# Routing attention with an activated FFN: cluster masks on VectorE and values in fours for half of the head pairs

## The chip, the cores and the metric

One NeuronCore of a Trainium2 chip runs the whole program. The metric is device time in microseconds, the median of several runs of the same kernel. Lower is better.

## What is computed

The attention block groups queries and keys of each head by their nearest centroid (16 per head) and lets a query see only keys of its own cluster. Its output, 3072 tokens of 512 features, goes through an FFN with a hard-swish. Everything is fp32.

```python
q_assign = np.argmax(np.einsum('bhsd,hcd->bhsc', q_n, c_n), axis=-1)      # B, H, S, D = 4, 8, 768, 64
k_assign = np.argmax(np.einsum('bhsd,hcd->bhsc', k_n, c_n), axis=-1)      # 16 clusters
mask = q_assign[:, :, :, None] == k_assign[:, :, None, :]
scores = np.where(mask, scale * np.matmul(q, k.transpose(0, 1, 3, 2)), -1000000000.0)
attn = np.exp(scores - np.max(scores, axis=-1, keepdims=True))
attn = attn / (np.sum(attn, axis=-1, keepdims=True) + 1e-09)
x = np.matmul(attn, v)                       # then (B, S, H*D) -> 3072 x 512
h = x @ w_in                                 # 512 x 2048
g = h * np.clip(h + 3.0, 0.0, 6.0) / 6.0
out = g @ w_out                              # 2048 x 512
```

## The kernel before

**Attention.** The 32 heads are handled as 16 pairs; the two heads of a pair (t = 0, 1) lie beside each other. A pair has 12 steps n: two halves hf of 384 queries, and in each half six chunks j of 128 keys. 192 steps in all, walked two at a time (r = n mod 12 is the place in the pair). A step's work:

- Scores (scores_part, L371). For each head the product of 128 keys and 384 queries over 64 features is laid on 64 of the array's rows, so the two heads lie side by side in the array; the result is keys by queries in one of two PSUM tiles ps. A second pair of bf16 matmuls, on the tile xm, adds the mask: xm holds one-hots of the query's cluster, and minus 2^60 for each cluster that is not the key's, so that a product over clusters is 0 for a match and minus 2^60 otherwise.
- Exponential (L387), ScalarE, from ps to a tile ex of 2 x 384 fp32 for both heads. Four buffers of ex.
- Key sums (L391, L394), GpSimd: the ex of the six chunks are added into acc. The first chunk of a half (j = 0) has no add.
- Values (attn_v, L398): v of the chunk times ex, each head on 64 columns of the array, accumulated over j in the one PSUM tile pv. After j = 5 ScalarE copies it to num (L410).
- Division (divide, L416) once a half: TensorE sums acc over the keys with a matrix of ones (pd, L425), VectorE takes the reciprocal (L429) and multiplies num (L430); what is stored of it and two ScalarE sums over it (in_range) wait in a list until the end of the next walk.

Values run two steps behind scores (lag_v = 2), so two values follow two scores in every walk. The tiles of the next pair are made during this one (prep_items, L680): three groups of transposes of q and k (turn), the products with the centroids (cluster_scores), their transposes and the one-hots by VectorE (route), and two groups of six transposes of one-hots that ScalarE copies to xm (route_turn). In the second half of the kernel all of these and pd share one PSUM buffer, that of the pool psum_t.

**FFN.** It runs by blocks of 256 tokens, 12 blocks. All but the first block's first product use a seven-product scheme of Strassen's kind on halves of the operands. A block has 15 items: eight ups (halved, L577) and seven downs (L629). An up makes seven partial products in two PSUM tiles, uX and uY, of a pool with two buffers; VectorE combines them (L603, L596, six instructions), ScalarE lifts (L453), VectorE clips (clip, L456), and after every second up four sums of the gated tiles are made by GpSimd, or by VectorE after the last (gated_sums, L575). The clip of an up is kept in the list ending and issued by finish() in the middle of the next up, between the work on uX and that on uY. In block 1 alone, first_sums (L507) makes four sums of w_in per up on VectorE; later blocks load them. A down is 16 matmul instructions of 256 columns or 32 in the first two; some end in adds to y on VectorE (L627).

**Order.** The order of every queue is written out by hand (manual_schedule, L717 on). In a walk come two scores, two values, a division where one is due, and then the fill: FFN items taken from a list, and between them the steps of the next pair's preparation, one after each item. items_by (L707) says how many FFN items should be done by step n: 8 by step 96, then 56 for every 48 steps. Up to step 96 (DECODED) VectorE and ScalarE also decode the weights beside the attention. After step 192 about 60 items are left, which run by themselves.

Of the kernel before, what the change touches and what calls it, by code (L numbers as in the profile page):

```python
# [17 lines left out]
C = 16  # L18
P = 128
# [97 lines left out]
def fast_path(ctx, tc, ok, q, k, v, centroids, moe_w_in, moe_w_out, out):  # L117
# [13 lines left out]
    rtp = pool("rtp", 1)  # L131
    smallp = pool("smallp", 1)
    expp = pool("expp", 4)
# [10 lines left out]
    decp = decoding.enter_context(tc.tile_pool(name="decp", bufs=2))  # L144
    psum_s = pool("psum_s", 2, space=PSUM)
# [20 lines left out]

    st = {}
    later = []

# [86 lines left out]
    cen = const.tile([P, D], F32, name="cen")  # L256
    parity = const.tile([P, 2], F32, name="parity")

    def constants():
# [10 lines left out]
        nc.gpsimd.memset(one_hot, 0.0)  # L270

# [4 lines left out]
    def centroid_norm():  # L276
        cn = unit_rows(nc, smallp, cen, D)
# [3 lines left out]
        wide = smallp.tile([P, 2, D], F32, name="cenwide")  # L281
# [40 lines left out]
    def route(g):  # L322
# [26 lines left out]
        later.append(count)  # L349

    def route_turn(g, part):
# [7 lines left out]
        nc.scalar.activation(out=dst, in_=po, func=ACT.Copy, scale=-FAR if part else 1.0)  # L359

# [10 lines left out]
    def scores_part(n, x, first):  # L371
        g, hf, j = where(n)
        for t in range(2):
            r = slice(t * D, (t + 1) * D)
            nc.tensor.matmul(  # L375
                st["ps", n][:, t, 0:HALF], lhsT=x[r, NCH + j],
                rhs=x[r, hf * NHC : (hf + 1) * NHC], start=first, stop=not first,
            )

    def scores(n):  # L380
        g, hf, j = where(n)
        if ("ps", n) not in st:
            scores_qk(n)
        scores_part(n, st["xm", g], False)
        sc = st.pop(("ps", n))[:, :, 0:HALF]
        ex = expp.tile([P, 2, HALF], F32, name="ex")
        nc.scalar.activation(out=ex, in_=sc, func=ACT.Exp, scale=SM_SCALE)  # L387
        st["ex", n] = ex
# [140 lines left out]
    def ffn_items(b):  # L529
# [47 lines left out]
        def halved(b, m, u, i, g):  # L577
# [28 lines left out]
            finish()  # L606
# [8 lines left out]
            lift(sx, g)  # L615
            ending.append(lambda: (clip(g, sx, g), gated_sums(i)))
# [63 lines left out]
    def prep_items(g, r):  # L680

        if g >= NPAIR:
            return []
        return {
            0: [lambda: turn(g, 0), lambda: turn(g, 1)],
            2: [lambda: turn(g, 2)],
            4: [lambda: cluster_scores(g)],
            6: [lambda: route(g)],
            8: [lambda: route_turn(g, 0)],
            10: [lambda: route_turn(g, 1)],  # L690
# [23 lines left out]
    fill, checks = [], []  # L714
    done = 0

    with tc.manual_schedule():  # L717
# [18 lines left out]
        for n in range(0, total + lag_d + 2, 2):  # L736
            g, r = divmod(n, per_pair)
            for i in (n, n + 1):
                if i < total:
                    scores(i)  # L740
            for i in (n - lag_v, n - lag_v + 1):
                if 0 <= i < total:
                    attn_v(i)
            m = n - lag_d + 1
            if m >= 0 and m % NCH == NCH - 1:
                later.append(divide(m))
# [416 lines left out]
```

## Time and profile before

| | |
|---|---|
| median of 3 runs | 1046.78 us (1046.28 to 1048.92) |
| the profiled execution: its own time | 1050.08 us |
| its span | 1048.3 us |
| steps 0 to 95 | to about 253 us |
| steps 96 to 191 | about 253 to 838 us |
| FFN items alone | about 838 us to the end |

| busy in the span | PE | PE weight loads | DVE | ACT | POOL |
|---|---|---|---|---|---|
| us | 1013.2 | 740.9 | 587.8 | 387.5 | 406.4 |

The stages are found by the starts of the exponentials. A row of the profile gives a line of the kernel, an engine, an operation and its tiles as output<-inputs. Rows of the timeline give start and duration in us; a row with x4 is four instructions in a row. A matmul row's duration reaches beyond the start of the next, since matmuls are pipelined: the pitch is read from the starts.

### The profile page before, as it was taken

To read this page: it belongs to the slowest core of one execution; us is meant where nothing else is said; L and a number is where in the kernel's file an instruction comes from. 1 tells how busy PE (TensorE), PEld (TensorE's weight loads), DVE (VectorE), ACT (ScalarE), POOL (GpSimd) and SP (SyncE) were. 2 spreads that over 40 slices of the span, in tenths; PEclk is the share of its full clock that TensorE was granted. 3 is DMA by queue.
4 is the path that set the end of the run, shared out by engine and by line. 5 is a ranking of instruction groups with operands and counts; after the bars stand their busy time and mean duration, and the time that the engine had idled before them with its cause. 6 is when DMAs were issued, how large, how long until landed. Compare 5 with 4: busy or idle time off the path is not lost.

```text
span 1048.3 us, 16637 instructions
## 1 busy us (share of the span) xinstructions
PE 1013.2 (97%) x6560; PEld 740.9 (71%) x6560; DVE 587.8 (56%) x1117; ACT 387.5 (37%) x764; POOL 406.4 (39%) x315
## 2 busy tenths in 40 slices
PE   8999989999998999999999999999999999999996
PEld 4444445546767778677777777777778798989995
DVE  4899987868477247246246345345245373727270
ACT  6888866674223233223223233233223111102010
POOL 3777657664234235135234235235334220303030
PEclk9999999999999999999999999999999999999999
DMA  6455554531043223223322232333032051414120
GB/s 164 107 141 142 161 143 111 141 84 46 31 118 104 54 81 89 53 66 84 73 71 88 64 89 64 71 94 96 3 91 86 1 144 34 142 42 140 51 61 25
DMA packets 107176, 90.34 MB, mean 86 GB/s; under 512 B 78416, under 2 KB 88656, under 8 KB 107088
## 3 DMA queue, kind: packets, MB, share of 16 engines
q1 hardware_dynamic: 106944, 89.15, 31.2%
q8 instruction: 54, 0.88, 0.3%
q14 instruction: 34, 0.28, 0.1%
q10 hardware_dynamic: 144, 0.03, 0.0%
HBM read 73.43 MB, written 15.73 MB: 85 GB/s over the span
## 4 chain that ended last, share of the span: by engine, by line
PE 76%; DVE 8%; ACT 2%; issue 1%; DMA 1%; SPq 1%; DVEq 0%; ACTq 0%
PE Y L620 16%; PE uY L585 13%; PE X L620 12%; PE ps L375 10%; PE uX L585 10%; PE pv L404 9%; PE ph L540 3%; DVE rcp L429 2%; PE pd L425 1%; DVE sx L596 1%; PE pqk L302 1%; DVE num L430 1%; DVE g_sb L456 1%; PE pcs L315 1%; SPq L191 1%
## 5 line engine op out<-in xcount | busy, mean ns | idle before, releaser
L394 POOL TENSOR_TENSOR acc<-acc,ex 128x768 f32<-128x768 f32 x128 | 239.6, 1872 | 226.8 <-ACT ex L387 220.9
L575 POOL TENSOR_TENSOR g_sb<-g_sb 128x256 f32<-128x256 f32 x144 | 105.9, 756 | 219.2 <-DVE g_sb L456 216.4
L453 ACT ACTIVATE sx<-g_sb,half_c 128x512 f32<-128x512 f32 x88 | 63.5, 722 | 304.7 <-DVE g_sb L596 304.7
L387 ACT ACTIVATE ex<-ps 128x768 f32<-128x768 f32 x192 | 146.4, 803 | 75.4 <-PE ps L375 75.1
L375 PE MATMUL ps<-xf 64*128 64x384 f32 x768 | 165.5, 509 | 4.0 <-ACT ex L387 4.0
L404 PE MATMUL pv<-ex,vt 128*64 128x384 f32 x768 | 145.1, 499 | 0.0
L391 POOL TENSOR_TENSOR acc<-ex 128x768 f32<-128x768 f32 x32 | 59.0, 1842 | 161.9 <-ACT ex L387 161.9
L429 DVE RECIPROCAL rcp<-pd 128x384 f32<-128x384 f32 x32 | 81.8, 2555 | 57.8 <-PE pd L425 57.8
L627 DVE TENSOR_TENSOR y<-y,Y 128x256 f32<-128x256 f32 x48 | 20.2, 420 | 157.8 <-PE Y L620 157.0
L404 PEld LDWEIGHTS pv<-ex,vt 128*64 128x64 f32 x768 | 46.6, 136 | 80.1 <-issue 75.8
L375 PEld LDWEIGHTS ps<-xf 64*128 64x128 f32 x768 | 63.1, 186 | 46.1 <-issue 28.8
L585 PE MATMUL uX<-xb,w_in_sb 128*128 128x128 f32 x704 | 93.8, 277 | 0.0
L620 PE MATMUL X<-w_out_sb,g_sb 128*128 128x256 f32 x384 | 91.4, 387 | 0.4 <-DVE sx L596 0.4
L620 PE MATMUL Y<-T,g_sb 128*128 128x256 f32 x384 | 87.6, 381 | 0.0
L620 PE MATMUL Y<-w_out_sb,g_sb 128*128 128x256 f32 x384 | 87.5, 381 | 0.0
L585 PEld LDWEIGHTS uX<-xb,w_in_sb 128*128 128x128 f32 x704 | 86.5, 194 | 0.0
L620 PEld LDWEIGHTS X<-w_out_sb,g_sb 128*128 128x128 f32 x384 | 71.9, 192 | 16.3 <-issue 6.1
L456 DVE SCALAR_TENSOR_TENSOR g_sb<-sx,g_sb 128x512 f32<-128x512 f32 x88 | 76.8, 873 | 8.8 <-ACT sx L453 8.8
L620 PEld LDWEIGHTS Y<-T,g_sb 128*128 128x128 f32 x384 | 72.0, 190 | 13.5 <-issue 4.2
L620 PEld LDWEIGHTS Y<-w_out_sb,g_sb 128*128 128x128 f32 x384 | 72.2, 190 | 13.0 <-issue 3.6
L603 DVE COPY sx<-uX 128x128 f32<-128x128 f32 x88 | 25.5, 290 | 84.5 <-PE uX L585 84.5
L375 PE MATMUL ps<-xm 64*128 64x384 bf16 x384 | 63.1, 323 | 3.1 <-ACT xm L359 2.8
(109 smaller groups left out, 1448.4 us busy)
## 6 DMA issues: line engine op xcount, KB each, us to landing
tx<-td SPq DMA_DIRECT2D x80, 384.0 KB, 3.2
raw<-in_moe_w_in_dram SPq DMA_DIRECT2D x16, 512.0 KB, 3.9
raw<-in_moe_w_out_dram SPq DMA_DIRECT2D x16, 512.0 KB, 3.7
qk<-in_q_dram SPq DMA_DIRECT2D x32, 192.0 KB, 4.6
qk<-in_k_dram SPq DMA_DIRECT2D x32, 192.0 KB, 4.8
vt<-in_v_dram SPq DMA_DIRECT2D x32, 192.0 KB, 4.4
xd<-num SPq DMA_DIRECT2D x32, 192.0 KB, 3.9
xb<-xd SPq DMA_DIRECT2D x12, 512.0 KB, 4.4
```

The costliest lines, as they stand in the source:

```text
L375: nc.tensor.matmul(st["ps", n][:, t, 0:HALF], lhsT=x[r, NCH + j], rhs=x[r, hf * NHC : (hf + 1) * NHC], start=first, stop=not first,)
L387: nc.scalar.activation(out=ex, in_=sc, func=ACT.Exp, scale=SM_SCALE)
L391: nc.gpsimd.tensor_tensor(out=acc, in0=st["ex", n - 1], in1=ex, op=ALU.add)
L394: nc.gpsimd.tensor_tensor(out=acc, in0=acc, in1=ex, op=ALU.add)
L404: nc.tensor.matmul(pv[t * D : (t + 1) * D], lhsT=vt[:, j, t], rhs=ex[:, t], start=(j == 0), stop=(j == NCH - 1),)
L429: nc.vector.reciprocal(out=rcp, in_=pd)
L453: nc.scalar.activation(out=r, in_=h, func=ACT.Relu, bias=half_c, scale=1.0 / 6.0)
L456: nc.vector.scalar_tensor_tensor(out=g, in0=r, scalar=1.0, in1=h, op0=ALU.min, op1=ALU.mult)
L540: nc.tensor.matmul(ph[:, t * HC : (t + 1) * HC], lhsT=w_in_sb[:, kt, f * P : (f + 1) * P], rhs=st["xb", b, m][:, kt], start=(kt == 0), sto ...
L575: eng.tensor_tensor(out=out_, in0=in0, in1=in1, op=op)
L585: nc.tensor.matmul(dst, lhsT=w[:, kt], rhs=x(kt), start=(kt == 0), stop=(kt == HK - 1))
L620: nc.tensor.matmul(bank[:, half * HC : (half + 1) * HC], lhsT=g_sb[:, kind, i], rhs=w[:, i], start=(first and i == 0), stop=(last and i == ...
```

## The change

For pairs 8 to 15 (MASKED = 8, steps 96 on):

- The bf16 mask matmuls are left out of the scores. After the exponential, two VectorE instructions per step (masks, one per head, 384 elements per partition, scalar_tensor_tensor) compare the query's cluster number with the key's and multiply ex by the result, in place. The key sums then read the masked ex.
- The numbers come from the one-hots (clusters): five VectorE instructions per pair. The tile xm holds query numbers in every row; spread makes it with 12 matmuls against a broadcast column and three ScalarE copies, where route_turn took 12 transposes and two copies.
- The walk is by fours (four_by_four). A walk with r = 2, 6, 10 has two scores, their exponentials and then the fill; its masks stay pending. A walk with r = 0, 4, 8 has two scores, exponentials, the pending masks and key sums, at r = 4 the division of the half before, then four values (and after the value with j = 5 its division), then the masks and key sums of its own two steps; it has no fill. At r = 8 the second exponential comes after the values.
- Preparation steps lie at r = 2, 6 and 10 only. The fill of a walk is thus that of four steps.
- finish() moves to the end of an up, behind the work on uY (all ups).
- ex has six buffers instead of four; some constants move to a pool that is closed with the decoding; GpSimd writes 16 small constants at the start.

```diff
--- before.py
+++ after.py
@@ -129,8 +129,9 @@
     vp = pool("vp", 2)
     xp = pool("xp", 2)
     rtp = pool("rtp", 1)
+    kidp = pool("kidp", 2)
     smallp = pool("smallp", 1)
-    expp = pool("expp", 4)
+    expp = pool("expp", 6)
     accp = pool("accp", 2)
     nump = pool("nump", 1)
     xnp = pool("xnp", 2)
@@ -142,6 +143,7 @@
     decoding = ctx.enter_context(ExitStack())
     rawp = decoding.enter_context(tc.tile_pool(name="rawp", bufs=2))
     decp = decoding.enter_context(tc.tile_pool(name="decp", bufs=2))
+    startp = decoding.enter_context(tc.tile_pool(name="startp", bufs=1))
     psum_s = pool("psum_s", 2, space=PSUM)
     psum_v = pool("psum_v", 1, space=PSUM)
     psum_t = pool("psum_t", 1, space=PSUM)
@@ -164,8 +166,10 @@
     counts = const.tile([P, 2, NPAIR], F32, name="counts")
     w_low = const.tile([P, 1], F32, name="w_low")
+    MASKED = NPAIR // 2
     st = {}
     later = []
+    numbers = []
     def scratch(shape, name, dtype=F32):
@@ -253,8 +257,10 @@
-    cen = const.tile([P, D], F32, name="cen")
+    cen = startp.tile([P, D], F32, name="cen")
     parity = const.tile([P, 2], F32, name="parity")
+
+    number = const.tile([P, C], BF16, name="number")
     def constants():
         make_identity(nc, ident)
@@ -268,17 +274,19 @@
         nc.gpsimd.memset(ones, 1.0)
         nc.gpsimd.memset(w_low, W_LOW)
         nc.gpsimd.memset(one_hot, 0.0)
+        for c in range(C):
+            nc.gpsimd.memset(number[:, c : c + 1], float(c))
         warm = psum_t.tile([P, 4, P], F32, name="warm", tag="t")
         for i in range(14):
             nc.tensor.transpose(out=warm[:, i % 4], in_=ident, identity=ident)
     def centroid_norm():
-        cn = unit_rows(nc, smallp, cen, D)
+        cn = unit_rows(nc, startp, cen, D)
         nc.scalar.activation(out=w_totals[:, 0, 0:1], in_=w_low, func=ACT.Exp)
-        wide = smallp.tile([P, 2, D], F32, name="cenwide")
+        wide = startp.tile([P, 2, D], F32, name="cenwide")
         for t in range(2):
             nc.vector.tensor_scalar_mul(out=wide[:, t], in0=cn, scalar1=parity[:, t : t + 1])
         st["wide"] = wide
@@ -347,6 +355,8 @@
                 )
         later.append(count)
+        if g >= MASKED:
+            numbers.append(lambda: clusters(g))
     def route_turn(g, part):
         if part == 0:
@@ -359,6 +369,40 @@
         nc.scalar.activation(out=dst, in_=po, func=ACT.Copy, scale=-FAR if part else 1.0)
+
+    def by_vector(n):
+        return where(n)[0] >= MASKED
+
+    def clusters(g):
+        oh = one_hot.rearrange("p j (t c) -> p j t c", t=2)[:, :, :, 0:C]
+        which = rtp.tile([P, NC2, 2, C], BF16, name="which")
+        nc.vector.tensor_tensor(
+            out=which, in0=oh, in1=number.unsqueeze(1).unsqueeze(1).to_broadcast([P, NC2, 2, C]), op=ALU.mult
+        )
+        qid = st["qid"] = rtp.tile([P, NCH, 2], BF16, name="qid")
+        kid = st["kid", g] = kidp.tile([P, NCH, 2], F32, name="kid")
+        nc.vector.tensor_reduce(out=kid, in_=which[:, NCH:], axis=AX.X, op=ALU.add)
+
+        nc.vector.tensor_scalar(
+            out=kid, in0=kid, scalar1=-1.0, scalar2=C * (C - 1) / 2.0, op0=ALU.mult, op1=ALU.add
+        )
+        qsum = rtp.tile([P, NCH, 2], F32, name="qsum")
+        nc.vector.tensor_reduce(out=qsum, in_=which[:, 0:NCH], axis=AX.X, op=ALU.add)
+        nc.vector.tensor_copy(out=qid, in_=qsum)
+
+    def spread(g, part):
+        if part == 0:
+            st["xm", g] = xp.tile([P, NC2, P], BF16, name="xm")
+        pb = scratch([P, 4, P], "pb")
+        for i in range(4):
+            t, j = divmod(4 * part + i, NCH)
+            nc.tensor.matmul(
+                pb[:, i], lhsT=st["qid"][:, j, t : t + 1].to_broadcast([P, P]), rhs=ident_q,
+                start=True, stop=True,
+            )
+        nc.scalar.copy(out=st["xm", g][:, 4 * part : 4 * part + 4], in_=pb)
+
+
     def where(n):
         g, r = divmod(n, 2 * NCH)
         return (g, *divmod(r, NCH))
@@ -374,18 +418,35 @@
             r = slice(t * D, (t + 1) * D)
             nc.tensor.matmul(
                 st["ps", n][:, t, 0:HALF], lhsT=x[r, NCH + j],
-                rhs=x[r, hf * NHC : (hf + 1) * NHC], start=first, stop=not first,
+                rhs=x[r, hf * NHC : (hf + 1) * NHC], start=first,
+                stop=not first or by_vector(n),
             )
     def scores(n):
-        g, hf, j = where(n)
         if ("ps", n) not in st:
             scores_qk(n)
-        scores_part(n, st["xm", g], False)
+        if not by_vector(n):
+            scores_part(n, st["xm", where(n)[0]], False)
+
+    def exponentials(n):
         sc = st.pop(("ps", n))[:, :, 0:HALF]
-        ex = expp.tile([P, 2, HALF], F32, name="ex")
+        ex = st["ex", n] = expp.tile([P, 2, HALF], F32, name="ex")
         nc.scalar.activation(out=ex, in_=sc, func=ACT.Exp, scale=SM_SCALE)
-        st["ex", n] = ex
+
+    def masks(n):
+        g, hf, j = where(n)
+        ex = st["ex", n]
+        for t in range(2):
+            nc.vector.scalar_tensor_tensor(
+                out=ex[:, t].rearrange("p (a b) -> p a b", b=P),
+                in0=st["xm", g][:, t * NCH + hf * NHC : t * NCH + (hf + 1) * NHC],
+                scalar=st["kid", g][:, j, t : t + 1], in1=ex[:, t].rearrange("p (a b) -> p a b", b=P),
+                op0=ALU.is_equal, op1=ALU.mult,
+            )
+
+    def key_sums(n):
+        g, hf, j = where(n)
+        ex = st["ex", n]
         if j == 1:
             acc = st["acc", g, hf] = accp.tile([P, 2, HALF], F32, name="acc")
             nc.gpsimd.tensor_tensor(out=acc, in0=st["ex", n - 1], in1=ex, op=ALU.add)
@@ -603,7 +664,6 @@
             nc.vector.tensor_copy(out=sx[:, 1], in_=X[:, 1])
             add(sx[:, 0], X[:, 0], sx[:, 1])
             add(sx[:, 2], X[:, 2], sx[:, 0])
-            finish()
             Y = psum_m.tile([P, 4, P], F32, name="uY", tag="m")
             part(Y[:, 0], tx[:, 0], s(0))
             part(Y[:, 1], wi(1, 0, i), a(1, 0))
@@ -613,6 +673,7 @@
             add(g[:, 3], Y[:, 0], sx[:, 2])
             add(g[:, 0:3], Y[:, 1:4], sx[:, 1:4])
             lift(sx, g)
+            finish()
             ending.append(lambda: (clip(g, sx, g), gated_sums(i)))
         def product(bank, half, kind, w, first, last, again, chunks=range(HF)):
@@ -677,17 +738,21 @@
-    def prep_items(g, r):
+
+    def prep_items(g, r, fours):
         if g >= NPAIR:
             return []
+        turns = [lambda part=part: turn(g, part) for part in range(3)]
+        one_hots = [lambda: route_turn(g, 0), lambda: route_turn(g, 1)]
+        if g >= MASKED:
+            one_hots = [lambda part=part: spread(g, part) for part in range(3)]
+        scores_of = [lambda: cluster_scores(g)]
+        ways = [lambda: route(g)]
+        if fours:
+            return {2: turns, 6: scores_of + ways, 10: one_hots}.get(r, [])
         return {
-            0: [lambda: turn(g, 0), lambda: turn(g, 1)],
-            2: [lambda: turn(g, 2)],
-            4: [lambda: cluster_scores(g)],
-            6: [lambda: route(g)],
-            8: [lambda: route_turn(g, 0)],
-            10: [lambda: route_turn(g, 1)],
+            0: turns[:2], 2: turns[2:], 4: scores_of, 6: ways, 8: one_hots[:1], 10: one_hots[1:],
         }.get(r, [])
     per_pair = 2 * NCH
@@ -711,8 +776,54 @@
         return up_first + (n - DECODED) * (per_ffn + 11) // per_batch
     st["early"] = st["free"] = True
-    fill, checks = [], []
-    done = 0
+    fill, checks, unmasked = [], [], []
+    st["done"], st["valued"] = 0, DECODED - lag_v
+
+    def check_all():
+        now, checks[:] = checks[:], []
+        for check in now:
+            check()
+
+    def ready(m):
+        if m % per_batch == per_batch - 1:
+            fill.extend(ffn_items(m // per_batch))
+
+    def four_by_four(n, r, steps):
+        for i in steps:
+            scores(i)
+        if r % 4 == 2:
+            for i in steps:
+                exponentials(i)
+            unmasked.extend(steps)
+            check_all()
+            for op in numbers:
+                op()
+            numbers.clear()
+            return
+
+
+        for i in steps[: 1 if r == 8 else 2]:
+            exponentials(i)
+        check_all()
+        for i in unmasked:
+            masks(i)
+            key_sums(i)
+        unmasked.clear()
+        if r == 4 or n >= total:
+            m = n - r % per_pair - 1 if n < total else total - 1
+            if ("acc", *where(m)[:2]) in st and m < st["valued"]:
+                later.append(divide(m))
+                ready(m)
+        for i in range(st["valued"], min(n, total)):
+            attn_v(i)
+            if i % per_pair == NCH - 1:
+                later.append(divide(i))
+        st["valued"] = min(n, total)
+        for i in steps[1 if r == 8 else 2 :]:
+            exponentials(i)
+        for i in steps:
+            masks(i)
+            key_sums(i)
     with tc.manual_schedule():
         nc.scalar.dma_start(cen, centroids.rearrange("h c d -> (h c) d"))
@@ -735,44 +846,53 @@
         for n in range(0, total + lag_d + 2, 2):
             g, r = divmod(n, per_pair)
-            for i in (n, n + 1):
-                if i < total:
+            fours = n >= DECODED
+            steps = [i for i in (n, n + 1) if i < total]
+            prep = prep_items(g + 1, r, fours)
+            if fours:
+                four_by_four(n, r, steps)
+            else:
+                for i in steps:
                     scores(i)
-            for i in (n - lag_v, n - lag_v + 1):
-                if 0 <= i < total:
-                    attn_v(i)
-            m = n - lag_d + 1
-            if m >= 0 and m % NCH == NCH - 1:
-                later.append(divide(m))
-            prep = prep_items(g + 1, r)
-            if r == 4 and prep:
-                prep.pop()()
+                    exponentials(i)
+                    key_sums(i)
+                for i in (n - lag_v, n - lag_v + 1):
+                    if i >= 0:
+                        attn_v(i)
+                m = n - lag_d + 1
+                if m >= 0 and m % NCH == NCH - 1:
+                    later.append(divide(m))
+                    ready(m)
+            if prep and r == (6 if fours else 4):
+                prep.pop(0)()
             if n == DECODED:
                 st["early"] = False
-            if m >= 0 and m % per_batch == per_batch - 1:
-                fill += ffn_items(m // per_batch)
             if r == 6:
                 load(g + 2, "q", "k")
                 load(g + 1, "v")
-            want = items_by(n + 2) - done
-            want = min(want, len(fill))
-            done += want
-            for i in range(max(len(prep), want)):
-                if i < want:
-                    fill.pop(0)()
-                if i < len(prep):
-                    prep[i]()
+            if not fours or r % 4 == 2 or n >= total:
+                want = min(items_by(n + 2) - st["done"], len(fill))
+                st["done"] += want
+                for i in range(max(len(prep), want)):
+                    if i < want:
+                        fill.pop(0)()
+                    if i < len(prep):
+                        prep[i]()
             for step in decode[: share[r]]:
                 step()
             del decode[: share[r]]
-            for check in checks:
-                check()
-            checks, later[:] = later[:], []
+            if not fours:
+                for op in numbers:
+                    op()
+                numbers.clear()
+                check_all()
+            checks.extend(later)
+            later.clear()
         while checks:
-            for check in checks:
-                check()
-            checks, later[:] = later[:], []
+            check_all()
+            checks.extend(later)
+            later.clear()
         for item in fill:
             item()
```

## The prediction

> **What bounds the kernel now.** First the page: busy shares and the 40 slices.
>
> ```profile
> PE 1013.2 (97%) x6560; PEld 740.9 (71%) x6560; DVE 587.8 (56%) x1117; ACT 387.5 (37%) x764; POOL 406.4 (39%) x315
> ...
> DVE  4899987868477247246246345345245373727270
> ```
>
> TensorE is full; VectorE is half free on average, but in waves (7 2 4 7 2 4): high in ups, low in downs. The busy times by stretch and TensorE's waits from 253 to 838 us, where the change acts:
>
> ```profile
> 253.00:838.00 585.00, 573.97 (x3727) 434.48 (x3725) 279.15 (x589) 174.31 (x320) 207.80 (x164) 0.99 0.26 71
> ```
>
> ```profile
> PE uX L585 <- DVE sx L596: 7.0, 8, 2.4
> PE pqk L302 <- DVE rcp L429: 2.0, 1, 2.0
> PE uY L585 <- DVE g_sb L596: 1.7, 4, 0.6
> PE X L620 <- DVE sx L596: 0.4, 1, 0.4
> ```
>
> Of 585 us TensorE works 574 and waits 11, always for VectorE. So at most its instructions and 11 us can go. One walk on TensorE (timeline; the pitch is the difference of starts):
>
> ```profile
> 588.48 0.92 PE L375 MATMUL ps<-xf 64*128 64x384 f32 x4
> 589.22 0.33 PE L375 MATMUL ps<-xm 64*128 64x384 bf16 x2
> 589.39 0.81 PE L375 MATMUL ps<-xf 64*128 64x384 f32 x4
> 590.03 0.33 PE L375 MATMUL ps<-xm 64*128 64x384 bf16 x2
> 590.29 1.51 PE L404 MATMUL pv<-ex,vt 128*64 128x384 f32 x8
> 591.73 0.48 PE L620 MATMUL Y<-w_out_sb,g_sb 128*128 128x256 f32 x1
> ```
>
> Scores take 0.64 us a step (589.39 to 590.03), a mask pair 0.17 (589.22 to 589.39), eight values 1.44 with the change of tile shape behind them. Each change of shape costs about 0.1: 0.74 instead of 0.64 at the start, 0.26 instead of 0.17 ahead of the values.
>
> Two VectorE rows decide the forecast, the tail of an up and an encounter with GpSimd:
>
> ```profile
> 573.99 0.29 DVE L596 TENSOR_TENSOR sx<-uY,sx 128x128 f32<-128x128 f32 x1 [0.22 <-PE uY L585]
> 574.19 0.75 DVE L596 TENSOR_TENSOR g_sb<-uY,sx 128x128 f32<-128x128 f32 x2
> 575.79 0.69 DVE L456 SCALAR_TENSOR_TENSOR g_sb<-sx,g_sb 128x512 f32<-128x512 f32 x1 [0.85 <-ACT sx L453]
> 576.51 4.67 DVE L575 TENSOR_TENSOR g_sb<-g_sb 128x256 f32<-128x256 f32 x4
> 576.53 4.04 POOL L394 TENSOR_TENSOR acc<-acc,ex 128x768 f32<-128x768 f32 x2 [2.18 <-ACT ex L387]
> ```
>
> TensorE ended that up at about 573.8; VectorE's work on uY lasts to 574.94, 1.15 later. The last row pair: four VectorE instructions take 4.67 us, though such a one takes 0.42 elsewhere (L526, L627). GpSimd's adds take 2.02 each instead of 1.81. They alternate: one VectorE instruction per add.
>
> And a long TensorE wait costs twice:
>
> ```profile
> 422.80 0.66 PE L302 MATMUL pqk<-ident,qk 128*128 128x128 f32 x4 [1.98 <-DVE rcp L429]
> 423.29 3.24 PE L620 MATMUL X<-w_out_sb,g_sb 128*128 128x256 f32 x8
> 426.32 2.27 PE L620 MATMUL X<-T,g_sb 128*128 128x256 f32 x8
> ```
>
> Eight such matmuls take 1.89 elsewhere; after the 1.98 us wait they lose 1.35 + 0.38. The 2.4 us wait at 325 us shows the same (about 1.4); one of 1.6 at 308 doesn't.
>
> [...]
>
> **The change, part by part.** Times below are from T, TensorE's end of a fill.
>
> *Removed:* 96 mask pairs of 0.163: **-15.6**. Shape changes per four steps: six before, four after; by the pitches 0.57 against 0.38: 0.195 x 24 = **-4.7**. Sum -20.3. Spread's 12 matmuls stand for route_turn's 12 transposes (pitch 0.056); a broadcast weight load isn't in the trace: 0 to 0.054 more each (the fp32 pitch 0.109), 84 of them, 0 to 4.5; no gain, as the columns are as many. I take 0. ScalarE: three copies of 0.57 for two of 0.80 per pair, hidden under the fill (ScalarE is 30% busy). The 16 constants: GpSimd has nothing from 2.8 to 17 us: 0. The first half is otherwise as it was: 0. SP's loads keep their order; what divide stores waits for one walk, and x of a batch is needed 20 steps later: 0.
>
> *Added on VectorE:* 192 masks. A clip of 512 takes 0.68 unlocked, so 384 give 0.55, with pitch 0.47; the other end is the clip's mean with locks, 0.905; below 0.4 nothing speaks for it. That is 96 to 174 us on an engine with 306 us free there: no bound on average. GpSimd makes the same 80 adds, a little later; its gated sums queue behind them, but the downs that read them come after the next values, so I take 0 (at worst one add, 1.8, in each of seven blocks). What counts is who waits on TensorE, in order.
>
> *Values.* The pending masks a, b (steps n-2, n-1) are queued behind the fill's VectorE work. If the fill ended in an up, that is uY to T+1.15 and, with finish() at the end, the earlier clip to T+1.8. Masks: a two, then b's first to T+3.3; the add of a begins, b's second waits for it, 1.8, and ends at T+5.5. TensorE comes to b's values at 0.1 + 1.28 + 0.09 + three values of 0.65 = T+3.5: **wait 2.0** at r = 0. At r = 4 pd (0.65) lies ahead: 1.4. At r = 8 step a has j = 0 and no add: none. items_by gives fills of 4, 5, 5 items; counted through, 7 up-ended ones lie before r = 0, 4 before r = 4 (one ends in up 7, whose clip and four sums come too: 3.8). Downs leave VectorE free early: none. 7 x 2.0 + 3 x 1.4 + 3.8 = **22**.
>
> *Spread.* At r = 8: pd ends at T+3.5, reciprocal to T+6.2, num to 6.7, three masks of the walk's own steps to 8.15, an add to 10.0, the last mask 10.35, then clusters, five instructions, about 1.3 by like rows (0.35 for 192 elements, 0.15 for small ones): T+11.7. TensorE: 4.8 after the values, 6.2 after two scores, first item to 9.4 to 9.75. Spread is next in TensorE's queue, and everything is behind it: 2.0 in four pairs, 2.8 in three where the item is an up whose uX is read late: **16**.
>
> *Block 1.* An up there costs VectorE 2.8 + 1.7 to 2.3 for first_sums, against 3.12 on TensorE; before, scores and values between gave it time, now five ups run in a row, with masks ahead: carried through, **7** beyond the above. *Others:* cluster_scores waits for the reciprocal that holds psum_t at r = 4, second ups for late uX: **5**.
>
> Waits 50 in place of 11: +39. Five are well over 2 us and bring the slow stretch, 5 x 1.5, less the two of before (3.1): +4. Sum -20.3 + 39 + 4 = **+22.7**: profiled execution 1050.1 to 1072.8; against the median, 3.3 lower, **1069.5**.
>
> **The rivals.** *The lock does not delay the masks* (0.25): GpSimd's adds come after the four, or give way. b ends at T+3.8, wait 0.3; spread about 0.2 to 0.6. Waits 16 for 11 (2 + 2, 3, 7, 2), no slow stretches: -20.3 + 5 - 3 = -18, **1028.5**; faster. It decides from new waits below 31 us, 1.3 per walk by four. For it: 306 us free, waves with room in downs. Against: the alternation above.
>
> *Masks at the locked mean* (0.10): 1.4 us later per four: 11 values and 7 spreads, +25, slow stretches +4: **1099**. For it: clip's 0.905; against: that mean holds the waits that I count apart.
>
> *In balance* (0.08): waits about 31 in all, **1047**: half of my waits hide behind each other. *It doesn't do what it says*: the loads of spread cost as much as the masks did; at most 4.5, so no case of its own.
>
> **Numbers.** Likeliest case 0.57, 1053 to 1086 (waits 33 to 65). With the others: range 1026 to 1088, which leaves out the slowest case and small tails. Faster by over 0.3% 0.25, within 0.3% (what a measurement can tell from none) 0.08, slower 0.67.
>
> **What would show it.** TensorE's waits: pv waiting for VectorE's ex, seven times about 2 us after fills that end in an up; pb waiting for qid about 2 us in seven pairs; mask instructions of 2 us beside acc adds. L375's bf16 rows at 192. Wrong: masks with a mean near 0.55 and pv without waits, then it is faster.

## The result and the profile after

The changed kernel takes 1094.95 us (median of 4 runs, 1086.85 to 1097.49) against 1047.55 in the same comparison: 1.0439 times the time before, 95% interval 1.0381 to 1.0497. The forecast was slower, 1069.5, with a range to 1088. The direction was right, the forecast amount about half of what came. The profiled execution has a span of 1091.6 us, 43.3 more than before.

The page of the changed kernel: busy time and granted clock, and the masks' group with its mean in ns.

```profile
PE 1021.4 (94%) x6368; PEld 749.5 (69%) x6368; DVE 750.8 (69%) x1349; ACT 387.5 (35%) x772; POOL 419.1 (38%) x331
...
PEclk9999999999989989989999999989999999999999
...
L440 DVE SCALAR_TENSOR_TENSOR ex<-xm,kid,ex 128x384 f32<-128x384 bf16 x192 | 170.9, 953 | 0.0
```

TensorE has 192 instructions fewer and is busy longer: a row's end is modelled, and below rows stretch over waits (14 values in 3.11 us) and slow clocks (1.91 for 1.06). The mean granted clock of the run is 0.976, before 0.994. A mask takes 0.953 us on average; its median in the trace is 0.612 and its shortest 0.604. The prediction's 0.55 was my estimate; the shortest row of 384 elements on num in the trace of before (L430) took 0.557. What TensorE's instructions waited for, 250 to 880 us (total, times, longest):

```profile
PE pb L399 <- DVE qid L391: 21.4, 7, 3.6
PE uX L646 <- DVE sx L657: 8.0, 9, 3.5
PE pv L465 <- DVE ex L440: 7.2, 8, 1.2
PE X L681 <- DVE sx L657: 2.9, 3, 2.2
PE pb L399 <- ACT xm L403: 1.0, 1, 1.0
```

And its weight loads, where the values' waits show better:

```profile
PEld pv L465 <- DVE ex L440: 26.0, 37, 1.9
```

**A wait of spread.** VectorE, GpSimd and TensorE of the changed kernel from the walk of r = 8 into that of r = 10:

```profile
467.69 3.75 DVE L440 SCALAR_TENSOR_TENSOR ex<-xm,kid,ex 128x384 f32<-128x384 bf16 x4
471.36 0.35 DVE L379 TENSOR_TENSOR which<-one_hot,number 128x384 bf16<-128x384 bf16 x1
471.74 0.35 DVE L384 TENSOR_REDUCE kid<-which 128x12 f32<-128x192 bf16 x1
472.13 1.31 DVE L386 TENSOR_SCALAR kid<-kid 128x12 f32<-128x12 f32 x1
473.36 0.34 DVE L390 TENSOR_REDUCE qsum<-which 128x12 f32<-128x192 bf16 x1
473.73 0.17 DVE L391 CAST qid<-qsum 128x12 bf16<-128x12 f32 x1
```

```profile
469.00 2.03 POOL L455 TENSOR_TENSOR acc<-acc,ex 128x768 f32<-128x768 f32 x1 [3.15 <-ACT rcp L503]
471.61 1.80 POOL L455 TENSOR_TENSOR acc<-acc,ex 128x768 f32<-128x768 f32 x1 [0.58 <-DVE ex L440]
```

```profile
470.08 0.61 PE L646 MATMUL uY<-xs,w_in_sb 128*128 128x128 f32 x4
473.96 0.61 PE L399 MATMUL pb<-ident_q,qid 128*128 128x128 bf16 x4 [3.27 <-DVE qid L391]
474.80 1.22 PE L646 MATMUL uX<-xs,tx 128*128 128x128 f32 x4 [0.23 <-DVE sx L657]
475.81 1.91 PE L646 MATMUL uX<-xb,w_in_sb 128*128 128x128 f32 x8
```

Four masks take 3.75 us: three take 0.61 each, the fourth, beside the first add, 2.16 (469.27 to 471.44). A VectorE instruction that lasts longer beside an add of GpSimd, as here, is all that "the lock" stands for in the prediction, the expectations and below. Then arithmetic on 12 numbers takes 1.31 us: it starts 0.5 us into the second add (471.61 to 473.41) and ends with it. TensorE stands 3.27 us, and what follows runs slowly: 1.22 and 1.91 us where the same rows take 0.71 and 1.06 elsewhere. The granted clock (third number from the end) is half there; after the last wait of spread, 2.86 us, it is full:

```profile
473.50:480.30 6.80, 6.11 (x30) 5.85 (x31) 2.88 (x11) 1.19 (x2) 0.00 (x0) 0.50 0.00 0
```

```profile
788.84 0.40 PE L399 MATMUL pb<-ident_q,qid 128*128 128x128 bf16 x4 [2.86 <-DVE qid L391]
```

```profile
788.80:800.00 11.20, 11.16 (x60) 9.77 (x61) 2.25 (x6) 2.03 (x4) 0.00 (x0) 1.00 0.01 2
```

**A wait of the values.** A walk of r = 0 after a fill that ended in an up:

```profile
566.55 1.56 PE L419 MATMUL ps<-xf 64*128 64x384 f32 x8
568.04 3.11 PE L465 MATMUL pv<-ex,vt 128*64 128x384 f32 x14
572.37 0.86 PE L465 MATMUL pv<-ex,vt 128*64 128x384 f32 x2 [1.22 <-DVE ex L440]
573.16 1.56 PE L419 MATMUL ps<-xf 64*128 64x384 f32 x8
```

```profile
567.53 1.12 DVE L517 SCALAR_TENSOR_TENSOR g_sb<-sx,g_sb 128x512 f32<-128x512 f32 x1
568.57 6.35 DVE L440 SCALAR_TENSOR_TENSOR ex<-xm,kid,ex 128x384 f32<-128x384 bf16 x6
```

```profile
569.85 2.05 POOL L455 TENSOR_TENSOR acc<-acc,ex 128x768 f32<-128x768 f32 x1 [1.75 <-ACT ex L434]
```

From 568.04 to 573.16 are 5.12 us for 16 instructions that need 16 x 0.1615 and a change of shape of 0.1, 2.68: 2.44 of wait, though the row admits only 1.22. The 0.1615 is the pitch where no value waits: in e3 (below) such 16 go from 560.02 to 562.71, 2.69. In the waits of this document that pitch is used.

**The sum by pitch.** For the second half (from the first exponential of step 96 to the first up of block 8) each run of TensorE's instructions is set against its count times its pitch: 585.8 us before, 626.0 after. With what lies outside:

| term | forecast | measured |
|---|---|---|
| mask matmuls and shape changes | -20.3 | -19.8 |
| values wait for masks | +22 | +28 |
| spread waits for qid | +16 | +23 |
| other waits, less those of before | 12 - 11 | -5 (what is left of the sum) |
| slow clock after long waits | +4 | +14 |
| outside the second half | 0 | +3 |
| sum | +22.7 | +43 |

The row of the other waits is a remainder and carries the errors of all rows above the sum.

**An eighth wait.** The forecast counts seven pairs and has nothing ahead of step 96. But the numbers of pair 8 are made there, beside pair 7, and its spread waits for them in the walk of r = 8. In VectorE's queue they stand behind sums of w_out:

```profile
242.67 0.61 PE L399 MATMUL pb<-ident_q,qid 128*128 128x128 bf16 x4 [4.05 <-DVE qid L391]
```

```profile
237.60 2.09 DVE L538 TENSOR_TENSOR T<-w_out_sb 128x1024 f32<-128x1024 f32 x1
239.61 1.95 DVE L379 TENSOR_TENSOR which<-one_hot,number 128x384 bf16<-128x384 bf16 x1
```

```profile
236.78 4.56 POOL L455 TENSOR_TENSOR acc<-acc,ex 128x768 f32<-128x768 f32 x2 [2.71 <-ACT ex L434]
```

The product for the numbers, which reads two tensors, takes 1.95 us beside the adds, 0.35 above. TensorE stands 4.05 us and has half the clock from 241.4 to 248.2. From the exponential of step 93 to that of step 96 the changed kernel takes 19.4 us, the kernel before 11.9: 7.5 more. Every trace with masks on TensorE has 11.9 there, every trace with masks on VectorE 17.7 to 19.7. The +3 of the table is these 7.5 less 4.7 by which this execution was ahead at step 93; part of that is a stretch of half clock at 147 us in the execution of before. e5, with the changed kernel's code up to there, has such a stretch too, so that part is chance.

### The profile page after: what moved, and what is told of

Same layout as the page of the kernel before. It is cut to its first block, busy times and chain, and to the rows that moved or that the text cites. A ratio compares the mean times of both kernels' runs of the same rounds, so it can differ in the third digit from the quotient of the medians.

```text
span 1091.6 us, 16543 instructions
## 1 busy us (share of the span) xinstructions
PE 1021.4 (94%) x6368; PEld 749.5 (69%) x6368; DVE 750.8 (69%) x1349; ACT 387.5 (35%) x772; POOL 419.1 (38%) x331
## 4 chain that ended last, share of the span: by engine, by line
PE 67%; DVE 23%; ACT 4%; DMA 3%; issue 2%; SPq 2%; DVEq 0%; ACTq 0%
PE Y L681 15%; PE uY L646 13%; PE X L681 11%; PE uX L646 10%; DVE ex L440 10%; PE ps L419 6%; PE pv L465 5%; DVE rcp L490 4%; PE ph L601 3%; SPq L195 1%; PE pqk L310 1%; DVE sx L657 1%; DVE num L491 1%; DVE g_sb L517 1%; DVE g_sb L657 1%
## 5 line engine op out<-in xcount | busy, mean ns | idle before, releaser
L455 POOL TENSOR_TENSOR acc<-acc,ex 128x768 f32<-128x768 f32 x128 | 248.4, 1940 | 209.0 <-DVE ex L440 126.1
L636 POOL TENSOR_TENSOR g_sb<-g_sb 128x256 f32<-128x256 f32 x144 | 109.8, 784 | 270.2 <-DVE g_sb L517 254.8
L440 DVE SCALAR_TENSOR_TENSOR ex<-xm,kid,ex 128x384 f32<-128x384 bf16 x192 | 170.9, 953 | 0.0
L465 PE MATMUL pv<-ex,vt 128*64 128x384 f32 x768 | 158.4, 500 | 9.8 <-DVE ex L440 8.5
L419 PE MATMUL ps<-xf 64*128 64x384 f32 x768 | 159.1, 513 | 2.8 <-ACT ex L434 2.8
L465 PEld LDWEIGHTS pv<-ex,vt 128*64 128x64 f32 x768 | 52.4, 137 | 103.2 <-issue 66.0
L646 PE MATMUL uX<-xb,w_in_sb 128*128 128x128 f32 x704 | 97.6, 284 | 0.0
L646 PEld LDWEIGHTS uX<-xb,w_in_sb 128*128 128x128 f32 x704 | 90.1, 200 | 0.0
L646 PE MATMUL uX<-xs,tx 128*128 128x128 f32 x352 | 59.2, 292 | 9.9 <-DVE sx L657 9.9
L517 DVE SCALAR_TENSOR_TENSOR g_sb<-sx,g_sb 128x512 f32<-128x512 f32 x88 | 66.6, 761 | 0.9 <-ACT sx L514 0.8
```

What stands on the lines that cost most here:

```text
L419: nc.tensor.matmul(st["ps", n][:, t, 0:HALF], lhsT=x[r, NCH + j], rhs=x[r, hf * NHC : (hf + 1) * NHC], start=first, stop=not first or by_v ...
L440: nc.vector.scalar_tensor_tensor(out=ex[:, t].rearrange("p (a b) -> p a b", b=P), in0=st["xm", g][:, t * NCH + hf * NHC : t * NCH + (hf + ...
L455: nc.gpsimd.tensor_tensor(out=acc, in0=acc, in1=ex, op=ALU.add)
L465: nc.tensor.matmul(pv[t * D : (t + 1) * D], lhsT=vt[:, j, t], rhs=ex[:, t], start=(j == 0), stop=(j == NCH - 1),)
L517: nc.vector.scalar_tensor_tensor(out=g, in0=r, scalar=1.0, in1=h, op0=ALU.min, op1=ALU.mult)
L636: eng.tensor_tensor(out=out_, in0=in0, in1=in1, op=op)
```

## The experiments

The theory after the result: a mask, or another VectorE instruction, takes longer beside GpSimd's adds (2.16 us for 0.61, 1.31 for 0.17), and at a few places TensorE's queue stands behind it; long waits bring slow stretches (half clock from 473.5 to 480.3 after 3.27 us). The rivals: VectorE is simply too full in the ups, wherever the work lies; or the walk by fours itself costs. Each run is compared with the kernel before on the same chip.

### e3: fours alone

```diff
-    MASKED = NPAIR // 2
+    MASKED = NPAIR
...
-        for t in range(2):
+        for t in range(2 if by_vector(n) else 0):
```

> Walks by fours, fill by fours, finish at the end of an up, six buffers of ex, but the masks stay on TensorE as before, so VectorE has no masks and no clusters. Theory: only the shape changes go (4.7 us) and a few waits for VectorE come or go: 1038 to 1047. Rival (it is the fill in fours, five ups in a row with VectorE's work piled up, that costs): 1060 or more.

Measured 1040.19 us, ratio 0.9937 (0.9914 to 0.9959), as expected. The fours are not what costs: without the masks the kernel is faster than before. So masks by VectorE, with clusters and spread, make 53 to 55 us (by the ratios and by the medians), after the 15.6 that they save. Even this kernel has one wait of 7.12 us for the same reason, VectorE and GpSimd beside each other:

```profile
561.44 7.75 DVE L636 TENSOR_TENSOR g_sb<-g_sb 128x256 f32<-128x256 f32 x4
569.12 2.54 DVE L490 RECIPROCAL rcp<-pd 128x384 f32<-128x384 f32 x1
```

```profile
558.55 8.42 POOL L455 TENSOR_TENSOR acc<-acc,ex 128x768 f32<-128x768 f32 x4
```

```profile
571.71 1.51 PE L323 MATMUL pcs<-xf,cnT 128*32 128x384 f32 x8 [7.12 <-DVE rcp L490]
```

Four sums of 0.42 us take 7.75, one add to each; the reciprocal that frees psum_t is queued behind them, and cluster_scores waits for that buffer.

### e2 and e12: no key sums

```diff
-        if j == 1:
+        if by_vector(n):
+            if j == 1:
+                acc = st["acc", g, hf] = accp.tile([P, 2, HALF], F32, name="acc")
+                nc.gpsimd.memset(acc, 1.0)
+        elif j == 1:
```

> GpSimd's key sums are left out from step 96 on (acc is filled with ones once a half, so the division is by a constant); everything else stands. Theory of the lock: masks take 0.55 us instead of 0.95, values wait 0.3 instead of 2 us at r = 0, qid is ready 2 us or more earlier; waits fall from about 60 to about 20 us and the slow stretches with them. Time 1030 to 1045. Rival (VectorE's own work, queued behind the fill, sets the waits, and the lock only lengthens instructions that nobody waits for): above 1075, with pv waiting as before.

> The kernel before without GpSimd's key sums from step 96 on (acc filled with ones once a half, the division is by a constant): the counterpart of e2. Theory: the kernel before has few VectorE instructions in the adds' way on TensorE's path, so 1040 to 1046, and nearly all of the 51 us that e2 gained over the changed kernel belong to the masks' encounter with the adds. Rival (the adds cost the kernel before as much): below 1030.

Both leave out the key sums from step 96 on and so compute something else; only their times are of use. e2: 1043.8 us, ratio 0.9972 (0.9960 to 0.9984), as expected. e12, the same in the kernel before: 1035.95, ratio 0.9907 (0.9881 to 0.9933), 4 us below what was expected. So the adds from step 96 on cost the changed kernel about 50 us and the kernel before about 10; some 40 of the 47 us between the two belong to the encounter of the change's VectorE work with them. That it goes through VectorE's own instructions, and not through GpSimd's work as such, is read from the durations: a mask takes 0.656 us on average in e2, 0.953 with the adds. In e2 the masks and spread's wait read

```profile
L440 DVE SCALAR_TENSOR_TENSOR ex<-xm,kid,ex 128x384 f32<-128x384 bf16 x192 | 113.5, 656 | 0.0
```

```profile
PE pb L399 <- DVE qid L391: 2.6, 7, 0.9
```

e2 is still 7 to 8 us behind e12, but not in the second half: from the first exponential of step 96 to the first up of block 8 it takes 572.6 us, e12 575.4. The difference is the eighth wait, 19.5 us against 11.9 between steps 93 and 96, since e2 still has its adds there. What is left to the rival of VectorE's own work are waits inside the half, where e2 should gain some 20 us by its fewer matmuls and gains 3. By pitch its values still wait 15 us. In walks of r = 0 it is 1.87 us where the last up had an even number, so that gated sums start on GpSimd just then, and at most 0.9 in the others; that these sums are the cause fits, but was not tried by itself.

### e1: clusters early

```diff
             check_all()
-            for op in numbers:
-                op()
-            numbers.clear()
             return
...
                     if i < len(prep):
                         prep[i]()
+            if fours and r == 6:
+                for op in numbers:
+                    op()
+                numbers.clear()
```

> The clusters of the next pair are made at the end of the fill at r = 6 instead of in the walk of r = 10; nothing else moves. Theory (places: TensorE waits at single points of VectorE's queue[...], and each long wait brings a slow clock): the seven waits of spread (23 us) go, and with them most of the slow stretches (10 to 15 us); two values walks may get 1.3 later. Time 1057 to 1068. Rival (VectorE is simply too full in the ups, so a wait that is taken away comes back at the next read of uX): 1085 or more. Rival (the slow clock doesn't come from these waits): 1072 to 1076, granted clock still 0.976.

Measured 1069.05, ratio 1.0227 (1.0194 to 1.0261), just above what was expected; granted clock 0.990. That is 22 to 26 us (ratios, medians) for one moved group of five small instructions per pair. The wait for qid is gone from step 96 on (the eighth, ahead of it, stays); of its 23 us and the slow stretches some came back as waits for uX:

```profile
PE uX L646 <- DVE sx L657: 14.2, 10, 3.5
PE pv L465 <- DVE ex L440: 9.8, 9, 1.7
```

The first had been 8.0. By pitch some 34 us went in the second half, 22 of waits for qid and 12 of slow clock, and some 8 came back, most of them at uX. So the clock does follow these waits (0.976 with them, 0.990 without), and the rival of a full VectorE holds for about a quarter.

### e5 and e9: qid first

```diff
         qid = st["qid"] = rtp.tile([P, NCH, 2], BF16, name="qid")
+        qsum = rtp.tile([P, NCH, 2], F32, name="qsum")
+        nc.vector.tensor_reduce(out=qsum, in_=which[:, 0:NCH], axis=AX.X, op=ALU.add)
+        nc.vector.tensor_copy(out=qid, in_=qsum)
         kid = st["kid", g] = kidp.tile([P, NCH, 2], F32, name="kid")
...
-        qsum = rtp.tile([P, NCH, 2], F32, name="qsum")
-        nc.vector.tensor_reduce(out=qsum, in_=which[:, 0:NCH], axis=AX.X, op=ALU.add)
-        nc.vector.tensor_copy(out=qid, in_=qsum)
```

> The changed kernel with one reordering in clusters: which, the sum for qid and its cast first, then the sum and the arithmetic for kid, which nobody waits for yet. In the changed kernel the arithmetic on 12 numbers takes 1.3 us, as it lies in the way of an add by GpSimd. Theory: qid is ready about 1.6 to 1.9 us earlier, the seven waits of spread fall from 3.1 to 3.7 to about 1.3 to 2[...]: 1070 to 1080, granted clock 0.985 or more. Rival (the cast takes the lock's wait in its place): waits above 2.5 us, 1090 or more.

A miss: 1091.02, ratio 1.0427 (1.0400 to 1.0454). The rival was right, the cast now takes what kid's arithmetic took, and that is back at 0.17:

```profile
471.65 1.31 DVE L385 CAST qid<-qsum 128x12 bf16<-128x12 f32 x1
472.87 0.34 DVE L387 TENSOR_REDUCE kid<-which 128x12 f32<-128x192 bf16 x1
473.25 0.17 DVE L389 TENSOR_SCALAR kid<-kid 128x12 f32<-128x12 f32 x1
```

e9 has no such instruction ahead of qid:

```diff
         qid = st["qid"] = rtp.tile([P, NCH, 2], BF16, name="qid")
+        with nc.allow_low_precision("small whole numbers"):
+            nc.vector.tensor_reduce(out=qid, in_=which[:, 0:NCH], axis=AX.X, op=ALU.add)
...
-        qsum = rtp.tile([P, NCH, 2], F32, name="qsum")
-        nc.vector.tensor_reduce(out=qsum, in_=which[:, 0:NCH], axis=AX.X, op=ALU.add)
-        nc.vector.tensor_copy(out=qid, in_=qsum)
```

> As e5 (the sum for qid ahead of kid's), but the sum is written straight to the bf16 tile qid, so no small one-input instruction stands between which and spread. In the changed kernel kid's arithmetic, in e5 the cast took 1.31 us there, waiting for an add by GpSimd. Theory: that wait is what made spread's wait 3.1 to 3.7 instead of the 2.0 forecast; without it (and without the second sum) about 1.3 to 1.9 is left, and the slow clock goes in most of the seven places: 1070 to 1080. Rival (something else holds qid): above 1086, waits above 2.5.

1081.08, ratio 1.0339 (1.0312 to 1.0366), just above what was expected. The wait fell as the theory says:

```profile
PE pb L398 <- DVE qid L384: 9.1, 7, 1.8
```

1.3 to 2.0 by pitch instead of 3.1 to 3.75. In the pairs where an up follows, kid's arithmetic then delays uX by 1.96, which keeps some slow stretches (granted clock 0.983).

### e4: masks by twos

```diff
-            fours = n >= DECODED
+            fours = False
...
                     exponentials(i)
+                    if by_vector(i):
+                        masks(i)
                     key_sums(i)
```

> Masks by VectorE in the second half, but walks by twos as before: two scores, exponentials, their masks and key sums, then values of the two steps before, then the fill. Values never meet fresh masks; the masks stand ahead of the fill's VectorE work, about 4 us with the lock, so that a fill that begins with ups waits about 1 us for uX. Theory: 15.6 us go from TensorE, 15 to 30 come back in waits for uX and in slow stretches: 1040 to 1065. Rival (VectorE too full in the ups wherever the masks lie): 1080 or more.

A miss for the theory as I had put it: 1106.21, ratio 1.0546 (1.0506 to 1.0586). Values don't wait, but the masks, 3.76 us in the walk at 597.55, stand ahead of the reciprocal, and psum_t stays held:

```profile
PE uX L646 <- DVE sx L657: 23.9, 19, 4.8
PE pqk L310 <- DVE rcp L490: 13.9, 7, 2.9
PE pb L399 <- DVE rcp L490: 11.9, 7, 4.7
```

Here the rival of the crowded engine and mine say the same: every place behind the masks in VectorE's queue that TensorE reads from is late. I had counted one such place and there were three.

### e6, e11 and e14: pending masks ahead of the last item

All three have e1's edit and this one:

```diff
                 for i in range(max(len(prep), want)):
+                    if i == want - 1:
+                        for u in unmasked:
+                            masks(u)
+                            key_sums(u)
+                        unmasked.clear()
                     if i < want:
```

> As e1 (clusters at the end of the fill at r = 6), and the pending masks and their key sums are issued ahead of the last item of the fill instead of in the walk of the values. TensorE reads nothing of that last item for the next 3 us, so VectorE's delay there is covered. Theory: the waits of values (24 us in the walks and 6 beside) go but for 2 to 5: 1040 to 1052. Rival (VectorE is too full in the ups: the time comes back at the next uX or in the walk's own masks): 1060 or more.

e6: 1053.48, ratio 1.0073 (1.0046 to 1.0099): 16 us better than e1, just above what was expected. e14 puts cluster_scores behind the second item as well; e11 also has finish() in the middle of an up again:

```diff
-            return {2: turns, 6: scores_of + ways, 10: one_hots}.get(r, [])
+            return {2: turns, 6: [lambda: None] + scores_of + ways, 10: one_hots}.get(r, [])
...
-            if prep and r == (6 if fours else 4):
+            if prep and not fours and r == 4:
```

> As e6 (clusters early, pending masks ahead of the last item of the fill), with the two edits of e10. Theory: e6 less the waits at cluster_scores (6 us) and the slow clock behind the longest: 1042 to 1048, so that masks by VectorE, 15.6 us of TensorE, still give back more than they save against e10, which has the masks on TensorE. Rival (masks pay once their places are right): 1030 or less.

> As e11 with finish() at the end of an up, so as e6 with cluster_scores after the second item. Theory (finish in the middle made e11 slow): 1042 to 1050. Rival (the later cluster_scores did): 1062 or more.

e14: 1049.11, ratio 1.0033 (1.0015 to 1.0051), as expected. e11: 1070.45, ratio 1.0252 (1.0213 to 1.0292), far off. In e11 TensorE waited 25.6 us in 11 places for exponentials, in one of them so:

```profile
565.69 0.59 PE L419 MATMUL ps<-xf 64*128 64x384 f32 x2 [3.55 <-ACT ex L434]
```

```profile
564.22 0.72 ACT L514 ACTIVATE sx<-g_sb,half_c 128x512 f32<-128x512 f32 x1 [7.66 <-DVE g_sb L657]
564.85 1.49 ACT L434 ACTIVATE ex<-ps 128x768 f32<-128x768 f32 x2
```

The exponentials are queued on ScalarE behind the lift of the last up, the lift needs VectorE's work on uY, and that is behind the masks and, with finish() in the middle, behind the clip too, 1.76 us there. The wait moved from values to scores.

### e7, e8, e10 and e13: finish and the place of cluster_scores

e7 is e3 with cluster_scores after the first item (the second edit above), e10 has it after the second, and finish() where it was:

```diff
             add(sx[:, 2], X[:, 2], sx[:, 0])
+            finish()
...
             lift(sx, g)
-            finish()
```

> As e3 (fours, masks on TensorE), and cluster_scores comes after the first item of the fill at r = 6 instead of ahead of it, so that it doesn't wait for the reciprocal. In e3 it waited 7.1 and 1.8 us there, behind four gated sums of VectorE that alternate with adds of GpSimd. Theory: 9 us of wait and some 2 of slow clock go: 1027 to 1034. Rival (the wait moves to the item after it): 1037 or more.

> As e7 (fours, masks on TensorE, cluster_scores later), with cluster_scores after the second item of the fill at r = 6 and finish() in the middle of an up as in the kernel before. Theory: the one wait of 3.7 us that e7 has left at cluster_scores goes, and finish gives 0 to 3: 1028 to 1034. Rival (both only move waits): 1035 to 1038.

e7: 1035.47, ratio 0.9893 (0.9871 to 0.9916), just over the range. e10: 1028.05, ratio 0.9836 (0.9810 to 0.9863), the fastest of all. TensorE's waits in e10's second half:

```profile
PE uX L646 <- DVE sx L657: 3.7, 4, 1.7
PE pv L465 <- ACT num L471: 0.5, 1, 0.5
```

Two more rows have 0.3 and 0.2.

e8 moves finish() alone, in the kernel before; e13 undoes that move in the changed kernel.

> The kernel before with finish() at the end of an up, nothing else. Theory: the adds on uY no longer stand behind the clip, so the small waits for uX and uY (7 and 1.7 us) shrink; 1042 to 1047. Rival (the later clip delays GpSimd's gated sums and what waits for them): 1050 or more.

> The changed kernel with finish() in the middle of an up, as in the kernel before; the clip no longer stands between the last uY and the pending masks. Theory (the masks start as soon as VectorE is done with the fill): values wait 0.5 to 0.7 less in 11 walks: 1084 to 1092. Rival (the clip in the middle meets GpSimd's gated sums, so the work on uY and with it masks and lifts come later, as in e11): 1098 or more.

e8: 1049.54, ratio 1.0025 (1.0003 to 1.0047), between theory and rival: the waits for uX didn't shrink. e13: 1086.25, ratio 1.0382 (1.0350 to 1.0415), 6 us less than the changed kernel by the ratios and 9 by the medians, with intervals that overlap. The forecast had the move at no cost of its own.

## Why the prediction was wrong in size

The mechanism was right (values and spread wait for VectorE's instructions, lengthened beside GpSimd's adds: 28 and 23 us by pitch), and three terms of the sum were mis-sized: the slow clock (4 forecast, 14 measured), spread (16, measured 23), and what lies ahead of step 96. The prediction set that at nothing ("The first half is otherwise as it was: 0"), and an eighth wait for qid cost 7.5 there.

- **What goes.** Right: 20.3 forecast, 19.8 by pitch; e3 and e10 show that the fours alone gain, and more than their shape changes, since the waits of before go too.
- **The lock.** Right in effect: e2 against e12 gives the encounter with the adds some 40 of the 47 us. The rival of masks free of it was wrong: their mean is 0.953 us, 0.656 without the adds.
- **Values.** Right in place, low in size: at r = 0 1.4 to 2.4 (forecast 2.0), at r = 4 3.83, 1.18, 1.31 and 1.18 (3.8 and 1.4). The rest up to 28 is the last walk, 2.8, which I had left out, and small waits at r = 4 and r = 8, set at none.
- **Spread.** The term that failed first: 23 instead of 16. The prediction's "clusters, five instructions, about 1.3 by like rows (0.35 for 192 elements, 0.15 for small ones)" took 2.54, from 471.36 to 473.90, since a small one took 1.1 us more beside an add. I had counted such waits only for instructions that read two tensors, like the four sums that took 4.67 us in the trace of before. In the changed kernel the sum for kid, which reads one, did run beside an add in its usual 0.35 in pairs 9 to 15, but kid's tensor_scalar took 1.31 there, and 0.17 in pair 8, where no add ran beside it; e5's cast shows the same (1.31 against 0.17). What sets these two apart from the sum was not shown. e9 without either ahead of qid has 1.3 to 2.0 of wait.
- **The slow clock.** The term that failed most: 4 forecast, 14 measured. I counted it for five waits well over 2 us; with 3.1 to 3.75 by pitch six of the seven waits of spread were followed by half clock, and each costs 1.4 to 3.3 us more. e1 takes these waits away and the granted clock goes from 0.976 to 0.990. Length alone doesn't tell: in the kernel before 1.98 us sufficed (half clock from 423.7 to 427.1), and 2.86, the last wait of spread in the changed kernel, brought nothing.
- **What decides it, by the traces.** Between 256 and 885 us the sixteen traces have 59 stretches of half clock. All last 3.41 or 6.83 us, and within a run they start whole multiples of 3.413 us apart (in the changed kernel at 313.06, 330.12 and 394.98: 5 and 19 of them). In the 3.41 us just ahead of each, TensorE stood 1.96 us or more (gaps over 0.4 us between starts are counted); of the 2814 other such pieces at full clock none had more than 2.34. In the traces of the two kernels alone it was 2.12 or more ahead of each of ten stretches and at most 2.09 in the 343 others. So, by these traces, it matters how much of one piece of this grid a wait fills, and thus where it lies.
- **Other waits.** The -5 is a remainder. TensorE's waits view has 11.9 us in the other places (8.0, 2.9, 1.0), against 11 before: +1, as forecast. That they came out lower is not shown.
- **finish().** Taken as part of T+1.8, with no cost of its own; e13 gives it 6 to 9 us with the masks behind it (not beyond the intervals), e8 some 3 without.
- **The heavier rival** (masks at the locked mean, 1099, at 0.10) came nearest in time: the mean is 0.953, but by waits that the likeliest case also held. Its own mechanism, 1.4 us more for every four, isn't what the trace shows: the values' waits at r = 0 are 2.0 on average, not 3.4.

Open: how much of what e2 still waits is GpSimd's gated sums, and what of the 21 us between e14 and e10 is the lock and what the order; nothing was run for these. Of the 21, 6.4 are the eighth wait, which e14 keeps, and 11 lie in the second half. Nor was the eighth wait moved by a run of its own.

## What to carry to other kernels

Work moved from the bound engine to one with idle time is priced not by that idle time but by what the bound engine next reads from the queue it joins: list each such read, and whose instructions lengthen the new ones: here a mask took 0.953 us on average with GpSimd's adds, 0.656 without. Look for the second half of a combined change that pays alone: here fours without masks gave 1.6% once the one buffer that they ran into was asked for later. And a wait of 2 us or more on the bound engine can cost nearly twice its length (the 1.98 us of before lost 1.73 more), as the clock may follow it: in the sixteen traces between 256 and 882 us half clock followed 10 of 23 waits of 2.0 to 2.3 us and 27 of 31 of 3 us or more, in the changed kernel's own trace 7 of 8 of the latter. Last, look at where a change starts to act, not only at the stage it is meant for: here the first pair's numbers were made ahead of step 96.

## What was not expected of the hardware

A VectorE instruction on 12 numbers took 1.31 us instead of 0.17 beside an add of GpSimd, though it reads only one tensor (kid's tensor_scalar; the cast in e5) and I had looked for this only where two are read. TensorE's rows ran at about half speed (1.91 for 1.06) for some 6 us (the stretched rows run from 474.8 to 480.6) after a wait of 3.27 us, and whether a wait was followed by half speed went by its length and by its place on a grid of 3.413 us.
